# A two-MLP attention kernel on one core: buffers of the second MLP and of the state rows placed by SBUF zones, the first forms moved into the state rows, two PSUM banks exchanged, the last block by rows

## The chip, the core and the metric

The kernel runs on one core of a Trainium2 chip. The metric is the device time of one execution in microseconds (us). Engine names are those of the profile: PE is the TensorE matmul, PEld its weight load, DVE is VectorE, ACT is ScalarE, SP is SyncE, whose queue (SPq) issues nearly all DMAs of this kernel, strictly in its order.

## What is computed

The reference is an attention between 512 token rows and 32 state rows per batch and head (8 batches, 8 heads of 64), then two MLPs over all 4608 rows (4096 token rows, 512 per batch, and 256 state rows, 32 per batch): the first with relu squared, the second with elu.

```python
    scores = scale * np.matmul(x, state.transpose(0, 1, 3, 2))
    a = softmax(scores)                                # over the 32 state rows
    xread = np.matmul(a, state)
    a2 = softmax(scale * np.matmul(state, x.transpose(0, 1, 3, 2)))   # over the 512 rows
    sread = np.matmul(a2, x)
    x = rows of concat([xread, sread])                 # 4608 x 512
    x = np.maximum(x @ w_in, 0.0) ** 2 @ w_out         # 512 -> 2048 -> 512
    h = x @ w_in2
    return np.where(h > 0.0, h, np.exp(np.minimum(h, 0.0)) - 1.0) @ w_out2
```

## The kernel before

Everything is kept transposed: features on the 128 partitions, rows along the free axis, a block being the 512 rows of one batch. An fp32 product is made of three fp32r matmuls, HI·LO, HI·HI and LO·HI, where a tile's HI part is a rounded copy (ACT, L163) and LO the remainder (DVE, L164); `split` makes both, and `mm3` or `product` issues the three (L158 to L160, or L43). TensorE is the engine that is nearly always busy.

The stages in order. Attention and the first MLP for six single blocks (`block`, L475 to L502): 16 steps, each with h = W1·x in one of two PSUM banks, relu and square on ACT, and two steps later four accumulations `acc`; at the block's end four copies `acc` to `o` in turn by ACT (L501) and DVE (L499), in two buffers, each followed by its DMA to `x2d` in DRAM (L502). `mp` (L329) are the small products that give a block its first operand, split into `m_..` tiles. Then one pair of blocks, 6 and 7 (`pair`, from L617): h of both in 32 steps, its banks alternating between two PSUM pools (`ps_y`, `ps_x`), then seven products with four fewer-than-eight sub-products (`out_products`, L47 to L101) whose weights `wr` are streamed by L614.

Then the state rows of the first MLP (L678 to L717): 256 columns, 16 steps `i` in a period each of 24 matmuls of 256 columns. A step makes h from `w1s[i]` (12 matmuls), relu (ACT L694), the square (DVE L696), the split `gs`, the split of `w1s[i+2]` (two ACT and two DVE operations), and two steps later 12 matmuls into `acc`. At the end four copies `acc` to `o` in two buffers (L714 DVE, L716 ACT), each with a DMA to `x2d[8]` (L717).

Then the second MLP in four pairs of blocks (n = 0 to 3). `load_xr` (L758) brings two blocks back from `x2d`, 1024 KB each; `x_forms` makes seven operands `xf` from them, each a split (ACT and DVE over 1024 columns), with four additions or subtractions on DVE (L776, L779, L784 and one more); `first_product` (L788 to L838) is made of groups of six matmuls named X, Y or Z, each with a weight tile `wr` of 256 KB brought by L751 out of a pool of 12; `second_product` follows by `out_products`. Last comes `state_block` (L882 to L930): the second MLP for the 256 state rows, `hs` and `as` products, the `as` accumulations over 8 steps `j`, then four copies to `o` in three buffers (ACT L929, DVE L927) and four DMAs to the output (L930).

The tile scheduler orders the instructions of every engine by their dependencies and the order written; each engine and SP's queue then run strictly in that order. Buffers come from pools: a tile that takes a buffer's place waits for the last use of what was there, the landing of a DMA out of it included, and a pool that is opened in the place of a closed one waits for the users of that part of SBUF or PSUM.

Of the kernel before, what the change touches and what calls it, by code (L numbers as in the profile page):

```python
# [9 lines left out]
F32 = mybir.dt.float32  # L10
F32R = mybir.dt.float32r
# [8 lines left out]
P = 128  # L20
# [9 lines left out]
NF = 7  # L30
# [74 lines left out]
def attn_mlp_kernel(ctx: ExitStack, tc: tile.TileContext, xt, xn, st, w1, v1, w2, v2, outx, outs):  # L105
# [63 lines left out]
    if True:  # L169
# [275 lines left out]
        w1s = {}  # L445

        def split_w1(f):
            t = at_p.tile([P, 2, KC, P], F32R, name=f"w1s{f}", tag=("t", "a2t")[f % 2])
            for c in range(2):
                sl = slice(2 * c, 2 * c + 2)  # L450
                split(t[:, HI, sl], t[:, LO, sl], w1_t[f // 4, c][:, :, (f % 4) * P:(f % 4 + 1) * P])
            w1s[f] = t
# [145 lines left out]
        single.close()  # L598


        double = one.enter_context(ExitStack())
        pool = pools(double)
        gq1_p = pool("gq1", FC)
# [2 lines left out]
        eu1_p = pool("eu1", 2)  # L606
        u21_p = pool("u21", 2)
        oo1_p = pool("oo1", 2)
        ps_x, ps_y, ps_z = [pool(n, 2, space=bass.MemoryType.PSUM) for n in ("psx1", "psy1", "psz1")]
        def weight1(j, f):  # L610
            t = wr1_p.tile([P, 2, 256], F32R, name="wr", tag="wr")
            src = {1: lambda: v1d[j][:, :, :256], 2: lambda: v1d[j + HF][:, :, :256],
# [4 lines left out]
        def pair(b0, bg):  # L617

            g = {q: [] for q in (11, 12, 21, 22)}
            for s in range(2 * FC):  # L620
                b, f = b0 + s // FC, s % FC
                ps = (ps_y, ps_x)[f % 2].tile([P, S], F32, name="h1", tag="yx"[f % 2])
                s1_x(b, ops[b], f, ps)
                t = g[(11, 12, 21, 22)[s // HF]]
                if f % 2 == 0:
                    t.append(gq1_p.tile([P, 2, S], F32, name="g1", tag="gq"))
                h = t[-1][:, f % 2]
                pace[:] = [nc.scalar.activation(out=h, in_=ps, func=AF.Relu)]
# [46 lines left out]
            pair(b, bg)  # L675


        v1s = {}  # L678

        def load_v1(f):  # L680
            if f < FC:
                v1s[f] = gq1_p.tile([P, 2, DM], F32R, name="v1s", tag="gq")
                nc.sync.dma_start(out=v1s[f].bitcast(F32), in_=v1d[f])

        for f in range(4):
            load_v1(f)
        op = operand_s()
        gs = {}
        for i in range(FC + LAG):
            if i < FC:  # L690
                ps = ps_x.tile([P, NST], F32, name="h", tag="x")
                s1_s(op, i, ps)
                r = eu1_p.tile([P, NST], F32, name="r", tag="eu")
                nc.scalar.activation(out=r, in_=ps, func=AF.Relu)  # L694
                g = u21_p.tile([P, NST], F32, name="g", tag="u2")
                nc.vector.tensor_tensor(out=g, in0=r, in1=r, op=ALU.mult)  # L696
                t = gs[i] = gp1_p.tile([P, 2, NST], F32R, name="gs", tag="gp")
                split(t[:, HI], t[:, LO], g)
                if i + 2 < FC:
                    split_w1(i + 2)  # L700
                load_v1(i + 4)
            f = i - LAG
            if f < 0:
                continue
            if f == 0:
                acc = [p.tile([P, NST], F32, name="acc", tag=c) for p, c in ((ps_y, "y"), (ps_z, "z")) for _ in range(2)]
            w, t = v1s.pop(f), gs.pop(f)
            for k in range(KC):
                sl = slice(k * P, (k + 1) * P)
                mm3(acc[k], (w[:, HI, sl], w[:, LO, sl]), (t[:, HI], t[:, LO]), f == 0, f == FC - 1)  # L710
        for k in range(KC):
# [3 lines left out]
            else:  # L715
                nc.scalar.activation(out=o, in_=acc[k], func=AF.Copy)  # L716
            nc.sync.dma_start(out=x2d[B][:, k], in_=o)  # L717
        double.close()
        one.close()


    pool2 = lambda name, bufs, **kw: ctx.enter_context(tc.tile_pool(name=name, bufs=bufs, reuse_waits="tile", **kw))
    xr_p = pool2("xr", 2)
    xf_p = pool2("xf", NF)
    wr_p = pool2("wr", 12)
    eu_p = pool2("eu", 5)
    u2_p = pool2("u2", 2)
    gq_p = pool2("gq", FC)
    gp_p = pool2("gp", 3)
    oo_p = pool2("oo", 3)  # L730
    ps_y = pool2("psy", 2, space=bass.MemoryType.PSUM)
    ps_z = pool2("psz", 3, space=bass.MemoryType.PSUM)
    ps_x = pool2("psx", 3, space=bass.MemoryType.PSUM)
    act, tt = nc.scalar.activation, nc.vector.tensor_tensor
    DM1, DM2 = slice(0, 2), slice(2, 4)

    def elu(h, out):

# [10 lines left out]
    def weight(name, j, f):  # L749
        t = wr_p.tile([P, 2, 256], F32R, name="wr", tag="wr")  # L750
        nc.sync.dma_start(out=t.bitcast(F32), in_=wf[name, j][:, f - 1])  # L751
        return t

    xf, xr = {}, {}

    def load_xr(b):
        xr[b] = xr_p.tile([P, KC, S], F32, name=f"xr{b}", tag="xr")
        nc.sync.dma_start(out=xr[b], in_=x2d[b])  # L758

    def x_forms(n):  # L760

        t1, t2 = xr[2 * n], xr[2 * n + 1]
        a11, a12, a21, a22 = t1[:, DM1], t1[:, DM2], t2[:, DM1], t2[:, DM2]

        def put(f, src):
            t = xf[n, f] = xf_p.tile([P, 2, 2, S], F32R, name=f"xf{n}_{f}", tag="xf")
            split(t[:, HI], t[:, LO], src)

        put(1, a11)
        yield  # L770
        put(2, a12)
        yield
        tt(out=a21, in0=a21, in1=a22, op=ALU.add)
        put(5, a21)
        yield
        tt(out=a11, in0=a21, in1=a11, op=ALU.subtract)  # L776
        put(6, a11)
        yield
        tt(out=a21, in0=a22, in1=a11, op=ALU.subtract)  # L779
        put(7, a21)  # L780
        yield
        put(4, a22)
        yield
        tt(out=a12, in0=a12, in1=a11, op=ALU.subtract)  # L784
        put(3, a12)
        yield

    def first_product(n, g):  # L788

# [76 lines left out]
    def prepare_s():  # L866

        raw = xr_p.tile([P, KC, NST], F32, name="xsr", tag="xr")
        nc.sync.dma_start(out=raw, in_=x2d[B])
        for i in range(2):  # L870
            load_plain(*order[i])
        yield
        xs[0] = xr_p.tile([P, 2, KC, NST], F32R, name="xs", tag="xr")
        split(xs[0][:, HI], xs[0][:, LO], raw)
        yield
        for i in range(4):
            split_plain(*order[i])
            if i + 2 < len(order):
                load_plain(*order[i + 2])
            yield  # L880

    def state_block(prepared):  # L882
# [14 lines left out]
        for i in range(HF + 2):  # L897
            if i < HF:
                w = plain.pop(("w2", i))
                ps = ps_x.tile([P, 2, NST], F32, name="hs", tag="x")  # L900
                for r in range(2):
                    for d in range(2):
                        sl = [slice(r * 256 + k * P, r * 256 + (k + 1) * P) for k in range(2)]
                        product(nc, ps[:, r], [(w[:, HI, d, x], w[:, LO, d, x]) for x in sl],
                                [(xs[0][:, HI, 2 * d + k], xs[0][:, LO, 2 * d + k]) for k in range(2)],
                                r == 1 and d == 1, r == 0 and d == 0)
                g = gq_p.tile([P, 2, NST], F32, name="gsf", tag="gq")
                elu(ps, g)
                t = gs[i] = gq_p.tile([P, 2, 2, NST], F32R, name="gss", tag="gq")
                split(t[:, HI], t[:, LO], g)  # L910
                refill()
            j = i - 2
            if j < 0:
                continue
            if j == 0:
                acc = [p.tile([P, NST], F32, name="as", tag=c) for p, c in ((ps_y, "y"), (ps_z, "z")) for _ in range(2)]
            w, t = plain.pop(("v2", j)), gs.pop(j)
            for r in range(2):
                for m in range(KC):
                    sl = slice(m * P, (m + 1) * P)  # L920
                    product(nc, acc[m], [(w[:, HI, r, sl], w[:, LO, r, sl])], [(t[:, HI, r], t[:, LO, r])],
                            j == HF - 1 and r == 1, j == 0 and r == 0)
            refill()
        for m in range(KC):
            o = oo_p.tile([P, NST], F32, name="o", tag="o")
            if m % 2:
                nc.vector.tensor_copy(out=o, in_=acc[m])  # L927
            else:
                act(out=o, in_=acc[m], func=AF.Copy)  # L929
            nc.sync.dma_start(out=outs[m * P:(m + 1) * P, :], in_=o)  # L930

    for b in range(2):
        load_xr(b)
    for _ in x_forms(0):
        pass
    for n in range(B // 2):
        g = {}
# [51 lines left out]
```

## Time and profile before

| | us |
|---|---|
| three runs | 1344.03, 1344.10, 1342.67; median 1344.03 |
| the profiled execution, its own time | 1342.72 |
| its span, first to last instruction | 1340.9 |
| PE busy in it | 1321.0 |
| mean granted clock of PE | 0.999 |

A row of the timeline has the start, the duration, the engine, the line, the operation, output and input tiles, and in brackets how long the engine was idle before it and what ended that. Matmuls overlap, so the cadence is read from starts: the 512-column ones follow each other by 0.227 us, the 256-column ones by 0.12 us.

### The profile page before, as it was taken

The numbers are of one execution on the slowest core, as the hardware profiler recorded it, in microseconds if no ns is written. First come the engines' busy times: TensorE is split into PE (matmuls) and PEld (weight loads), VectorE is DVE, ScalarE is ACT, GpSimd is POOL, SyncE is SP. The second block draws the span as 40 slices with busy tenths as digits, with TensorE's granted clock in tenths as the row PEclk, the third lists the DMA queues.
The fourth block names the chain that finished last, engine by engine and source line by source line (L and its number), as shares of the span: only waits on it lengthen the run. The fifth ranks groups of instructions, "written<-read, shape, count | busy, mean of one in ns | idle before, by whom it ended". The sixth has DMA issues, their size and how long they took to land.

```text
span 1340.9 us, 19689 instructions
## 1 busy us (share of the span) xinstructions
PE 1321.0 (99%) x7064; PEld 1056.0 (79%) x7064; DVE 914.5 (68%) x1373; ACT 836.6 (62%) x1417; POOL 0.7 (0%) x6
## 2 busy tenths in 40 slices
PE   8999999999999999999999999999999999999998
PEld 6567777777677777788978888888888888888898
DVE  6986758686867645775476974579646884568644
ACT  5996657776766547654466743676446843666444
POOL 0000000000000000000000000000000000000000
PEclk9999999999999999999999999999999999999999
DMA  7998866676765203488086777678777677778733
GB/s 272 318 303 318 308 239 235 249 280 221 283 230 212 97 24 103 141 269 311 9 294 195 224 240 238 193 194 260 219 225 193 208 208 223 209 211 279 227 107 100
DMA packets 127729, 290.72 MB, mean 217 GB/s; under 512 B 13840, under 2 KB 22032, under 8 KB 124560
## 3 DMA queue, kind: packets, MB, share of 16 engines
q1 hardware_dynamic: 127632, 289.46, 66.4%
q8 instruction: 56, 0.92, 0.3%
q14 instruction: 41, 0.34, 0.1%
HBM read 212.86 MB, written 76.55 MB: 216 GB/s over the span
## 4 chain that ended last, share of the span: by engine, by line
PE 88%; ACT 3%; DMA 3%; DVE 3%; issue 1%; SPq 0%; DVEq 0%; ACTq 0%
PE x L43 16%; PE X L43 13%; PE z L43 8%; PE Z L43 6%; PE acc L158 6%; PE acc L160 6%; PE acc L159 6%; PE h L158 4%; PE h L159 4%; PE y L43 4%; PE h L160 4%; PE Y L43 3%; PE mp L329 2%; PE hs L43 2%; PE as L43 2%
## 5 line engine op out<-in xcount | busy, mean ns | idle before, releaser
L163 ACT ACTIVATE gp<-g 128x1024 fp32r<-128x1024 f32 (+1 forms) x168 | 153.9, 916 | 144.0 <-PE x L43 68.4
L164 DVE TENSOR_TENSOR gp<-g,gp 128x1024 fp32r<-128x1024 f32 (+1 forms) x168 | 175.0, 1046 | 96.0 <-ACT gp L163 94.3
L43 PE MATMUL x<-gp,wr 128*128 128x512 f32 x960 | 223.6, 390 | 0.0
L43 PEld LDWEIGHTS x<-gp,wr 128*128 128x128 f32 x960 | 179.6, 188 | 39.6 <-ACT eu L71 1.9
L43 PE MATMUL X<-xf,wr 128*128 128x512 f32 x768 | 186.6, 390 | 0.0
L43 PEld LDWEIGHTS X<-xf,wr 128*128 128x128 f32 x768 | 143.4, 188 | 31.6 <-ACT u L746 1.3
L158 PE MATMUL acc<-gs,v 128*128 128x512 f32 x384 | 155.0, 404 | 3.6 <-DVE gs L472 3.6
L160 PE MATMUL acc<-gs,v 128*128 128x512 f32 x384 | 150.3, 391 | 0.0
L159 PE MATMUL acc<-gs,v 128*128 128x512 f32 x384 | 149.9, 390 | 0.0
L43 PE MATMUL z<-gp,wr 128*128 128x512 f32 x480 | 110.4, 389 | 0.0
L742 DVE SCALAR_TENSOR_TENSOR g<-r,g 128x512 f32<-128x512 f32 x96 | 63.9, 689 | 65.8 <-ACT r L741 65.8
L158 PE MATMUL h<-at,m 128*128 128x512 f32 x256 | 102.1, 399 | 3.0 <-ACT r L467 1.9
L43 PEld LDWEIGHTS z<-gp,wr 128*128 128x128 f32 x480 | 90.1, 188 | 18.7
L158 PEld LDWEIGHTS acc<-gs,v 128*128 128x128 f32 x384 | 72.0, 188 | 40.9 <-issue 15.9
L159 PE MATMUL h<-at,m 128*128 128x512 f32 x256 | 100.6, 393 | 0.0
L160 PE MATMUL h<-at,m 128*128 128x512 f32 x256 | 99.7, 391 | 0.0
L467 ACT ACTIVATE r<-h 128x512 f32<-128x512 f32 x96 | 57.3, 597 | 64.5 <-PE h L160 64.3
L43 PE MATMUL Z<-xf,wr 128*128 128x512 f32 x384 | 97.4, 389 | 0.0
L740 ACT ACTIVATE r<-g 128x512 f32<-128x512 f32 x96 | 57.5, 625 | 57.5 <-DVE g L819 40.4
L472 DVE TENSOR_TENSOR gs<-g,gs 128x512 fp32r<-128x512 f32 x96 | 66.1, 689 | 29.5 <-ACT gs L471 28.5
L160 PEld LDWEIGHTS acc<-gs,v 128*128 128x128 f32 x384 | 72.1, 188 | 17.3 <-issue 1.7
L159 PEld LDWEIGHTS acc<-gs,v 128*128 128x128 f32 x384 | 72.2, 188 | 15.2 <-issue 1.7
(142 smaller groups left out, 2137.5 us busy)
## 6 DMA issues: line engine op xcount, KB each, us to landing
wr<-f_v SPq DMA_DIRECT2D x256, 256.0 KB, 3.1
wr<-f_w SPq DMA_DIRECT2D x224, 256.0 KB, 3.0
f_v<-wf SPq DMA_DIRECT2D x40, 512.0 KB, 3.4
raw_w<-in_w_dram SPq DMA_DIRECT2D x32, 512.0 KB, 5.1
raw_v<-in_v_dram SPq DMA_DIRECT2D x32, 512.0 KB, 5.1
f_w<-wf SPq DMA_DIRECT2D x24, 512.0 KB, 3.3
xt<-in_xt_dram SPq DMA_DIRECT2D x8, 1024.0 KB, 7.8
xn<-in_xn_dram SPq DMA_DIRECT2D x8, 1024.0 KB, 5.9
```

What stands on the lines that cost most here:

```text
L43: nc.tensor.matmul(ps, wk[a], xk[b], start=start and k == 0 and i == 0, stop=last and k == len(w) - 1 and i == 2, skip_group_check=True)
L158: mm(ps, w[HI], x[LO], start=first, stop=False)
L159: mm(ps, w[HI], x[HI], start=False, stop=False)
L160: mm(ps, w[LO], x[HI], start=False, stop=last)
L163: copy = nc.scalar.activation(out=hi, in_=src, func=AF.Copy)
L164: nc.vector.tensor_tensor(out=lo, in0=src, in1=hi.bitcast(F32), op=ALU.subtract)
L329: mm(ps[e][32 * k:32 * k + 32, :], st_t[b][r, k, :], x(k, r), start=True, stop=True)
L467: pace[:] = [nc.scalar.activation(out=r, in_=ps, func=AF.Relu)]
L472: nc.vector.tensor_tensor(out=gs[:, LO], in0=g, in1=gs[:, HI].bitcast(F32), op=ALU.subtract)
L740: act(out=r, in_=h, func=AF.Relu, scale=-1.0)
L742: nc.vector.scalar_tensor_tensor(out=out, in0=r, scalar=-1.0, in1=h, op0=ALU.add, op1=ALU.max)
```

## The change

Four things are done.

1. Pools. `w1s` of the state rows gets a pool of its own at the right end of SBUF, opened before the pair, instead of two buffers of the attention; the state rows get a stage `rows` with own pools (`eu2`, `u22`, `oo2`, six `v1s` buffers instead of the pair's sixteen, `gs` in the `m` buffers; PSUM pools in the order y, x, z). The second MLP's pools are opened in another order, `xr`, `xf` and `gp` at the right end.
2. `load_xr(0)`, `load_xr(1)` and the seven steps of `x_forms(0)` are called inside the loop over the state rows, a form at every second step from i = 4; before they stood behind that loop.
3. The pair's h goes to `ps_z` and `ps_y`, and its PSUM pools are opened as y, x, z instead of x, y, z.
4. In the last step j of `state_block` the loop runs by rows of the output: all six matmuls of `acc[0]`, then those of `acc[1]`, and so on; `o` takes buffers of the `eu` pool (5) instead of `oo` (3).

```diff
         def split_w1(f):
-            t = at_p.tile([P, 2, KC, P], F32R, name=f"w1s{f}", tag=("t", "a2t")[f % 2])
+            t = w1s_p.tile([P, 2, KC, P], F32R, name=f"w1s{f}", tag="w1s")
...
+        w1s_p = right("w1s", 2)
         double = one.enter_context(ExitStack())
...
-        ps_x, ps_y, ps_z = [pool(n, 2, space=bass.MemoryType.PSUM) for n in ("psx1", "psy1", "psz1")]
+        ps_y, ps_x, ps_z = [pool(n, 2, space=bass.MemoryType.PSUM) for n in ("psy1", "psx1", "psz1")]
...
-                ps = (ps_y, ps_x)[f % 2].tile([P, S], F32, name="h1", tag="yx"[f % 2])
+                ps = (ps_z, ps_y)[f % 2].tile([P, S], F32, name="h1", tag="zy"[f % 2])
...
+        double.close()
+        xr_p = right("xr", 2)
+        xf_p = right("xf", NF)
+        rows = one.enter_context(ExitStack())
+        v1_p = rows.enter_context(tc.tile_pool(name="v1s", bufs=6, side="right", reuse_waits="tile"))
+        pool = pools(rows)
+        eu1_p = pool("eu2", 2)
+        u21_p = pool("u22", 2)
+        oo1_p = pool("oo2", 2)
+        ps_y, ps_x, ps_z = [pool(n, 2, space=bass.MemoryType.PSUM) for n in ("psy2", "psx2", "psz2")]
...
+        for b in range(2):
+            load_xr(b)
+        forms = x_forms(0)
         for i in range(FC + LAG):
...
-                t = gs[i] = gp1_p.tile([P, 2, NST], F32R, name="gs", tag="gp")
+                t = gs[i] = m_p.tile([P, 2, NST], F32R, name="gs", tag="m")
...
+            if i > 3 and i % 2 == 0:
+                next(forms, None)
...
-        double.close()
+        rows.close()
         one.close()
...
+    pool = pools(ctx)
+    xs_p = pool("xs", 1)
+    gq_p = pool("gq", FC)
+    eu_p = pool("eu", 5)
+    oo_p = pool("oo", 3)
+    u2_p = pool("u2", 2)
+    wr_p = pool("wr", 12)
+    gp_p = right("gp", 3)
...
-            for r in range(2):
-                for m in range(KC):
-                    sl = slice(m * P, (m + 1) * P)
...
+            last = j == HF - 1
+            for i in range(2 * KC):
+                r, m = (i % 2, i // 2) if last else divmod(i, KC)
...
-            o = oo_p.tile([P, NST], F32, name="o", tag="o")
+            o = eu_p.tile([P, NST], F32, name="o", tag="eu")
```

What stands in a row on TensorE where the pair begins: `acc` is the last accumulation of block 5, `mp6_1` the operand products of block 6, `h1` the first h of the pair. Before:

```order
L160 MATMUL acc_4531<-gs_5091,v1_15_1068 128x512
L329 MATMUL mp6_1_0_5208<-w1_10_318,st6_3894 32x512 [waits PE_49]
L329 MATMUL mp6_1_1_5209<-w1_10_318,st6_3894 32x512 [waits PE_49]
L329 MATMUL mp6_1_0_5208<-w1_10_318,st6_3894 32x512
L329 MATMUL mp6_1_1_5209<-w1_10_318,st6_3894 32x512
L329 MATMUL mp6_1_0_5208<-w1_11_373,st6_3894 32x512
L329 MATMUL mp6_1_1_5209<-w1_11_373,st6_3894 32x512
L329 MATMUL mp6_1_0_5208<-w1_11_373,st6_3894 32x512
L329 MATMUL mp6_1_1_5209<-w1_11_373,st6_3894 32x512
L158 MATMUL h1_5189<-at6_4722,m6_00_4984 128x512 [waits Activation_49]
```

The same place after the change:

```order
L160 MATMUL acc_4531<-gs_5091,v1_15_1068 128x512
L158 MATMUL h1_5196<-at6_4722,m6_00_4984 128x512
L159 MATMUL h1_5196<-at6_4722,m6_00_4984 128x512
L160 MATMUL h1_5196<-at6_4722,m6_00_4984 128x512
L158 MATMUL h1_5196<-at6_4722,m6_01_4987 128x512
L159 MATMUL h1_5196<-at6_4722,m6_01_4987 128x512
L160 MATMUL h1_5196<-at6_4722,m6_01_4987 128x512
L329 MATMUL mp6_1_0_5215<-w1_10_318,st6_3894 32x512 [waits PE_49]
L329 MATMUL mp6_1_1_5216<-w1_10_318,st6_3894 32x512 [waits PE_49]
L158 MATMUL h1_5206<-at6_4722,m6_00_4984 128x512 [waits Activation_49]
L159 MATMUL h1_5206<-at6_4722,m6_00_4984 128x512
```

The first h now stands ahead of the operand products and waits for no copy; the second stands between two of the products and the remaining six, and waits for ACT.

What stands in a row on SP where the state rows end and the second MLP begins: `x2d8` are the four DMAs of the state rows' `o`, `wr` the weights of `first_product` for n = 0, `xr2` and `xr3` the blocks of n = 1. Before:

```order
L751 DMA wr_7015<-f_w20_2009 128x512 [waits DMAHW2_49,DVE_49]
L751 DMA wr_7026<-f_w20_2009 128x512 [waits DMAHW3_49,DVE_49,PE_49]
L751 DMA wr_7040<-f_w20_2009 128x512 [waits DMAHW4_49]
L751 DMA wr_7048<-f_w20_2009 128x512 [waits DMAHW5_49]
L751 DMA wr_7059<-f_w21_2056 128x512 [waits DMAHW6_49]
L717 DMA x2d8_131<-o_6912 128x256 [waits DMAHW7_49,Activation_49]
L717 DMA x2d8_131<-o_6915 128x256 [waits DMAHW0_49,DVE_49]
L751 DMA wr_7069<-f_w20_2009 128x512 [waits DMAHW1_49]
L751 DMA wr_7080<-f_w21_2056 128x512 [waits DMAHW2_49]
L751 DMA wr_7094<-f_w21_2056 128x512 [waits DMAHW3_49]
L717 DMA x2d8_131<-o_6918 128x256 [waits DMAHW4_49,Activation_49]
```

After:

```order
L697 DMA xr2_7044<-x2d2_125 128x2048 [waits DVE_49,Activation_49]
L697 DMA xr3_7046<-x2d3_126 128x2048 [waits DVE_49,Activation_49]
L771 DMA x2d8_131<-o_6984 128x256 [waits DMAHW4_49,Activation_49]
L771 DMA x2d8_131<-o_6987 128x256 [waits DMAHW5_49,DVE_49]
L771 DMA x2d8_131<-o_6990 128x256 [waits DMAHW6_49,Activation_49]
L771 DMA x2d8_131<-o_6993 128x256 [waits DMAHW7_49,DVE_49]
L803 DMA wr_7053<-f_w20_2009 128x512 [waits DMAHW0_49]
L803 DMA wr_7064<-f_w20_2009 128x512 [waits DMAHW1_49]
L803 DMA wr_7078<-f_w20_2009 128x512 [waits DMAHW2_49]
```

All weights of the second MLP now stand behind the four DMAs of the state rows' `o`; before, five stood ahead of them and three more between the second and the third.

What stands in a row on TensorE at the same place. Before:

```order
L160 MATMUL acc<-gs,v1s 128x256
L43 MATMUL Y<-xf_2_6984,wr 128x512 [waits DMAHW3_49,DVE_49,PE_49]
L43 MATMUL Y<-xf_2_6984,wr 128x512 [waits Activation_49]
L43 MATMUL Y<-xf_2_6984,wr 128x512 x4
L43 MATMUL Z<-xf_5_6988,wr 128x512 [waits DMAHW4_49,DVE_49]
L43 MATMUL Z<-xf_5_6988,wr 128x512 [waits Activation_49]
L43 MATMUL Z<-xf_5_6988,wr 128x512 x4
L43 MATMUL Y<-xf_2_6984,wr 128x512 [waits DMAHW2_49,PE_49]
L43 MATMUL X<-xf_1_6981,wr 128x512 x6
```

After:

```order
L160 MATMUL acc<-gs,v1s 128x256
L43 MATMUL X<-xf_1_6512,wr 128x512 [waits DMAHW0_49]
L43 MATMUL X<-xf_1_6512,wr 128x512 x5
L43 MATMUL Y<-xf_2_6593,wr 128x512 [waits DMAHW1_49,PE_49]
L43 MATMUL Y<-xf_2_6593,wr 128x512 x5
L43 MATMUL Z<-xf_5_6675,wr 128x512 [waits DMAHW2_49,Activation_49]
```

The first group is now X, and it waits for a weight's DMA alone; before, the first Y also waited for the forms on DVE and ACT.

## Rows read from the trace of the kernel before

**Rows 1.** Page of the profile: busy us, share of the span, instructions by engine.

```profile
PE 1321.0 (99%) x7064; PEld 1056.0 (79%) x7064; DVE 914.5 (68%) x1373; ACT 836.6 (62%) x1417; POOL 0.7 (0%) x6
```

**Rows 2.** Waits of PE: what for, us in total, times, the longest.

```profile
PE Y L43 <- DMA wr<-f_w: 1.9, 1, 1.9
```

**Rows 3.** Timeline where the pair begins: PE and ACT.

```profile
497.87 0.60 ACT L501 ACTIVATE o<-acc 128x512 f32<-128x512 f32 x1 [3.63 <-PE acc L160]
...
499.80 1.09 PE L329 MATMUL mp<-w,st 64*32 64x512 f32 x16
501.14 0.60 ACT L501 ACTIVATE o<-acc 128x512 f32<-128x512 f32 x1 [2.68 <-DMA x2d<-o]
...
501.79 0.51 PE L158 MATMUL h<-at,m 128*128 128x512 f32 x1 [0.90 <-ACT o L501]
```

**Rows 4.** Timeline of PE: operand products, then an acc that follows them.

```profile
479.15 1.09 PE L329 MATMUL mp<-w,st 64*32 64x512 f32 x16
480.17 0.50 PE L158 MATMUL acc<-gs,v 128*128 128x512 f32 x1
```

**Rows 5.** Groups by line, 660 to 690; count, busy us, mean ns.

```profile
L164 DVE TENSOR_TENSOR xf<-xr,xf 128x1024 fp32r<-128x1024 f32 x7 | 8.4, 1220 | 2.3 <-ACT xf L163 2.3
...
L163 ACT ACTIVATE xf<-xr 128x1024 fp32r<-128x1024 f32 x7 | 7.2, 1051 | 0.5 <-DVE xr L776 0.3 <-DVE xr L779 0.2
```

**Rows 6.** Window in the state rows: busy us of PE, PEld, DVE, ACT, POOL.

```profile
640.00:660.00 20.00, 20.00 (x169) 20.00 (x168) 10.02 (x28) 9.10 (x28) 0.00 (x0) 1.00 0.05 14
```

**Rows 7.** Timeline of the state rows' end: PE.

```profile
674.34 0.28 PE L160 MATMUL acc<-gs,v1s 128*128 128x256 f32 x1
...
674.82 0.39 PE L158 MATMUL acc<-gs,v1s 128*128 128x256 f32 x1 [0.20 <-DVE gs L164]
```

**Rows 8.** Timeline of SP's queue there.

```profile
675.89 0.80 SPq L717 DMA_DIRECT2D x2d<-o  x2
```

**Rows 9.** Timeline into the second MLP: ACT, DVE and PE.

```profile
675.48 0.38 ACT L716 ACTIVATE o<-acc 128x256 f32<-128x256 f32 x1
...
675.84 0.42 DVE L714 COPY o<-acc 128x256 f32<-128x256 f32 x1
...
676.36 1.55 PE L43 MATMUL Y<-xf,wr 128*128 128x512 f32 x6
...
677.92 0.39 ACT L716 ACTIVATE o<-acc 128x256 f32<-128x256 f32 x1 [2.06 <-PE Y L43]
...
681.20 0.47 PE L43 MATMUL Y<-xf,wr 128*128 128x512 f32 x1 [1.93 <-DMA wr<-f_w]
```

**Rows 10.** Timeline of PE: first products: n = 0's end, then n = 1's.

```profile
758.10 2.20 PE L43 MATMUL x<-gp,wr 128*128 128x512 f32 x9
...
831.61 1.52 PE L43 MATMUL X<-xf,wr 128*128 128x512 f32 x6
...
910.96 2.43 PE L43 MATMUL x<-gp,wr 128*128 128x512 f32 x10
```

**Rows 11.** DMA issues, 655 to 657: us to landing with no other transfer.

```profile
wr<-f_w SPq DMA_DIRECT2D x1, 256.0 KB, 2.7
```

**Rows 12.** Windows: busy us of PE, PEld, DVE, ACT, POOL; granted clock; DMA.

```profile
2.00:3.00 1.00, 1.00 (x6) 1.00 (x6) 0.00 (x0) 0.01 (x1) 0.00 (x0) 1.00 0.65 233
...
7.00:8.00 1.00, 1.00 (x10) 1.00 (x9) 0.00 (x0) 0.00 (x0) 0.00 (x0) 1.00 0.91 315
...
679.00:681.20 2.20, 0.27 (x2) 0.03 (x1) 2.20 (x4) 2.00 (x3) 0.00 (x0) 1.00 0.97 331
...
1339.00:1340.00 1.00, 0.00 (x0) 0.00 (x0) 0.00 (x0) 0.00 (x0) 0.00 (x0) 0.50 0.39 131
```

**Rows 13.** Timeline of the end.

```profile
1335.77 0.88 PE L43 MATMUL as<-gss,pl 128*128 128x256 f32 x6
...
1336.02 2.62 SPq L930 DMA_DIRECT2D out_dram<-o  x4
...
1337.86 0.42 DVE L927 COPY o<-as 128x256 f32<-128x256 f32 x1 [1.46 <-DMA out_dram<-o]
```

More of the change, by code (lines that the diff above doesn't have):

```diff
@@ L598, in attn_mlp_kernel @@
         single.close()
+        right = lambda name, bufs: ctx.enter_context(tc.tile_pool(name=name, bufs=bufs, side="right", reuse_waits="tile"))
+        right("edge", 1).tile([P, 8], F32, name="edge", tag="edge")
+        w1s_p = right("w1s", 2)
         double = one.enter_context(ExitStack())
@@ L675, in attn_mlp_kernel, with load_xr, x_forms, put @@
             pair(b, bg)
+        double.close()
[8 more added lines that the diff above has]
+        ps_y, ps_x, ps_z = [pool(n, 2, space=bass.MemoryType.PSUM) for n in ("psy2", "psx2", "psz2")]
+        xf, xr = {}, {}
+        DM1, DM2 = slice(0, 2), slice(2, 4)
+        def load_xr(b):
+            xr[b] = xr_p.tile([P, KC, S], F32, name=f"xr{b}", tag="xr")
+            nc.sync.dma_start(out=xr[b], in_=x2d[b])
+        def x_forms(n):
+            t1, t2 = xr[2 * n], xr[2 * n + 1]
+            a11, a12, a21, a22 = t1[:, DM1], t1[:, DM2], t2[:, DM1], t2[:, DM2]
+            def put(f, src):
+                t = xf[n, f] = xf_p.tile([P, 2, 2, S], F32R, name=f"xf{n}_{f}", tag="xf")
+                split(t[:, HI], t[:, LO], src)
+            put(1, a11)
+            yield
+            put(2, a12)
+            yield
+            nc.vector.tensor_tensor(out=a21, in0=a21, in1=a22, op=ALU.add)
+            put(5, a21)
+            yield
+            nc.vector.tensor_tensor(out=a11, in0=a21, in1=a11, op=ALU.subtract)
+            put(6, a11)
+            yield
+            nc.vector.tensor_tensor(out=a21, in0=a22, in1=a11, op=ALU.subtract)
+            put(7, a21)
+            yield
+            put(4, a22)
+            yield
+            nc.vector.tensor_tensor(out=a12, in0=a12, in1=a11, op=ALU.subtract)
+            put(3, a12)
+            yield
         v1s = {}
@@ L681, in load_v1 @@
             if f < FC:
-                v1s[f] = gq1_p.tile([P, 2, DM], F32R, name="v1s", tag="gq")
+                v1s[f] = v1_p.tile([P, 2, DM], F32R, name="v1s", tag="v1s")
                 nc.sync.dma_start(out=v1s[f].bitcast(F32), in_=v1d[f])
@@ L717, in attn_mlp_kernel @@
             nc.sync.dma_start(out=x2d[B][:, k], in_=o)
-        double.close()
+        rows.close()
         one.close()
[L722 to L733, printed above, removed]
+    pool = pools(ctx)
[6 more added lines that the diff above has]
+    gp_p = right("gp", 3)
+    ps_y = pool("psy", 2, space=bass.MemoryType.PSUM)
+    ps_z = pool("psz", 3, space=bass.MemoryType.PSUM)
+    ps_x = pool("psx", 3, space=bass.MemoryType.PSUM)
     act, tt = nc.scalar.activation, nc.vector.tensor_tensor
-    DM1, DM2 = slice(0, 2), slice(2, 4)
     def elu(h, out):
@@ L752, in weight @@
         return t
[L754 to L786, printed above, removed]
     def first_product(n, g):
@@ L872, in prepare_s @@
         yield
-        xs[0] = xr_p.tile([P, 2, KC, NST], F32R, name="xs", tag="xr")
+        xs[0] = xs_p.tile([P, 2, KC, NST], F32R, name="xs", tag="xs")
         split(xs[0][:, HI], xs[0][:, LO], raw)
@@ L917, in state_block @@
             w, t = plain.pop(("v2", j)), gs.pop(j)
-            for r in range(2):
-                for m in range(KC):
-                    sl = slice(m * P, (m + 1) * P)
-                    product(nc, acc[m], [(w[:, HI, r, sl], w[:, LO, r, sl])], [(t[:, HI, r], t[:, LO, r])],
-                            j == HF - 1 and r == 1, j == 0 and r == 0)
+            last = j == HF - 1
+            for i in range(2 * KC):
+                r, m = (i % 2, i // 2) if last else divmod(i, KC)
+                sl = slice(m * P, (m + 1) * P)
+                product(nc, acc[m], [(w[:, HI, r, sl], w[:, LO, r, sl])], [(t[:, HI, r], t[:, LO, r])],
+                        last and r == 1, j == 0 and r == 0)
             refill()
         for m in range(KC):
-            o = oo_p.tile([P, NST], F32, name="o", tag="o")
+            o = eu_p.tile([P, NST], F32, name="o", tag="eu")
             if m % 2:
@@ L930, in state_block @@
             nc.sync.dma_start(out=outs[m * P:(m + 1) * P, :], in_=o)
-    for b in range(2):
-        load_xr(b)
-    for _ in x_forms(0):
+    for _ in forms:
         pass
```

## The prediction, made before the changed kernel was run

> **What bounds the kernel now.** I read the busy times first: TensorE is busy for 1321.0 of 1340.9 us [rows 1], so only two things count, TensorE's work, which the change leaves as it is, and TensorE's idle places. The list of PE's waits says which of these the change reaches: the largest is 1.9 us for a weight `wr` of the second MLP [rows 2], and a copy `o` holds it for 0.9 [rows 3]. The timeline then gives each place: where the pair begins [rows 3], where the state rows end [rows 7 to 9] and the kernel's last microseconds [rows 13]. DVE and ACT matter only where they are ahead of one of these.
>
> **The pair's first h.** Before, the operand products `mp` start at 499.80 and take 16 slots; the next such run, 479.15 to 480.17, shows 1.02 us to the matmul behind it [rows 4], so h could have started at 500.82. It started at 501.79, because its bank waited for ACT's second `o`, which itself waited for a DMA out of the first [rows 3]: 0.97 us lost. After, the first h goes to a bank that no copy holds and stands ahead of `mp`; the second waits for the `o` of 497.87, done at 498.48, long before. The late copy then holds up a later h that is not yet wanted. Against this: `mp` is now broken in two, one more switch between the two kinds of matmul. The `acc` behind such a run lasts 0.50 [rows 4], 0.27 over a slot of 0.227; I count 0.3. ACT also gets the splits of `w1s[0]` and `[1]` here, four of some 0.4 us, which may cost a later h as much as one of them. I take a gain of 0.5, between 0 (both eat it) and 0.97.
>
> **The state rows.** Seven forms and two loads come in among 16 periods. A period of 24 matmuls at 0.12 us is 2.88 us. DVE was busy 10.02 and ACT 9.10 of 20 us there [rows 6], so 1.44 and 1.31 us of a period: about half is free. The forms need of DVE seven splits and four additions at 1.22 us, 13.4 us, and of ACT seven at 1.05, 7.4 us [rows 5]. They come in eight periods, 23.0 us: ACT 7.4 + 8 × 1.31 = 17.9 fits; DVE 13.4 + 8 × 1.44 = 24.9 overflows by 1.9 us. That backlog costs TensorE nothing as long as `gs` has slack: h of step i is wanted as `gs` two periods later, 5.76 us, of which the chain of relu, square and the two halves of the split takes four operations of about 0.4, so some 4 us are left. The two loads of 1024 KB have the DMA engines nearly to themselves, 0.05 busy in that window [rows 6]. So I put the forms at nothing, covered by DVE's free half; what they cost when that cover is gone is the second rival. What they save is one stall: at 674.82 an `acc` waited for a `gs` that stood behind a form of 1.22 us on DVE [rows 7]. The matmul before it started at 674.34 [rows 7] in a cadence of 0.12: 0.48 − 0.12 = 0.36 us. The forms are done by then after the change: −0.36.
>
> **Into the second MLP.** Here the change moves most, and not the way its placement reads. Before, the first Y starts at 676.36, the slot after the last `acc`; call it T0 [rows 9]. PE idles 1.93 us at 681.20 for a weight. The whole cost of the transition: from T0 to the same `x` group the first product takes 758.10 − 676.36 = 81.74 us, for n = 1 it takes 910.96 − 831.61 = 79.35 [rows 10], so 2.39 us.
>
> After, all `wr` stand behind the four DMAs of the state rows' `o` on SP's queue, and SP executes in order. The `o` have two buffers, so the third and fourth copies wait for the first and second DMA to land. I take these times from the same place in the trace. The first copy starts at 675.48, its DMA is issued at 675.89 [rows 8, 9], and ACT's next copy starts at 677.92: 2.03 us from issue to reuse; at the kernel's end the same chain takes 1337.86 − 1336.02 = 1.84 [rows 13]. The second copy runs from 675.84 to 676.26 on DVE; its issue starts at about 676.30. The fourth copy, on DVE, can therefore start 1.84 to 2.03 us later, at 678.14 to 678.33, and takes 0.42; its issue takes SP 0.3 to 0.4 (two took 0.80 [rows 8]), so SP comes to the first `wr` at 678.9 to 679.2. A `wr` of 256 KB alone lands 2.7 us after issue [rows 11]. TensorE gets its first X at 681.6 to 682.0: idle for 5.2 to 5.6 us from T0, and I take 5.4. Later weights are issued every 0.4 us [rows 8] and wanted every 1.36 (six matmuls of 0.227), so I expect no second wait. The difference is 5.4 − 2.39 = **+3.0 us** (2.8 to 3.3).
>
> **The clock after that gap.** With TensorE idle for 1.93 us the granted clock stayed at 1.00; after the last matmul of the kernel it was 0.50, the low level (1.2 GHz), by 1339 [rows 12], the last matmul having ended at 1336.65 [rows 13]. At the kernel's start, out of idleness, six idle matmuls went by in the microsecond from 2, ten in that from 7 [rows 12]; the recorded clock is 1.00 in both, so I go by the counts. If all of 1 to 7 ran at 0.6 of the rate, 6 × 0.4 = 2.4 us were lost; at half rate 3.0. After the gap the same loss, or none if the clock holds: 0 to 3.0. I take 2.4, because the start is the only restart that this trace has.
>
> The Trainium skill speaks against the change here: in its page "TensorE: Matmul & The Clock Gate", section "HAM oscillation — how this bites in real kernels", a TensorE left waiting for DMAs falls to half rate and the burst behind the wait starts cold. Its example has 1.67 us of throttled time for each such wait, by an estimate from that page 0.84 us lost, with which the time would be 1345.2. The clock of 0.50 at the end of the trace agrees; a restart behind a gap in the middle is not in it.
>
> **The last block.** The last matmul ends at 1336.65, but the fourth copy waited for a landing until 1337.86 [rows 13]. With free buffers and the first three copies ended by then (`acc[0]` now ends 18 matmuls earlier instead of 9) the fourth starts at about 1336.7, and its DMA lands that much earlier: −1.17, between −1.0 and −1.2.
>
> **Everything else** I put at nothing: six `v1s` buffers instead of sixteen still load four steps ahead, 11.5 us, and the DMA engines are free there [rows 6]; other pools and zones change addresses; the pair's seven products take their banks in another order, without a wait that this trace shows near. What would cost is a late transfer, in the second rival.
>
> **The sum.** −0.5 − 0.36 + 3.0 − 1.17 = +1.0 us, and with the clock's 2.4, **+3.4**. The profiled execution took 1342.72 and the median of three is 1344.03; I add to the middle of the two, 1343.4: **1346.8**.
>
> **Rivals.**
> - *The clock holds through the gap.* For: 1.93 us of idling left it at 1.00 [rows 12]; a low stretch might be short too. Against: 0.50 at the end of the trace. It gives 1343.4 + 1.0 = 1344.4, not slower.
> - *DVE falls behind in the state rows, on top of the gap: slower still.* The backlog of 1.9 us leaves about 2 us of slack. If the forms come in closer than one in a period, or if an operand block lands late and holds everything behind it on DVE's queue, TensorE loses each microsecond beyond that slack. From about 4 us of backlog it decides; at 2 us beyond, 1348.7. For: DVE in order, and the additions wait for the loads. Against: the DMA engines' emptiness [rows 6].
> - *The change does what its placement reads as: weights and forms are there when the state rows end.* Then the 2.39 us vanish too: −0.5 − 0.36 − 2.39 − 1.17 = −4.4, so 1339.0, faster. It needs `wr` issued before the third and fourth `o`, or their DMAs much quicker than 1.84 us. Against: the order of SP's queue, printed above. This is where I would be most wrong.
>
> **How the numbers follow.** A measurement of this kernel can tell about 0.2%, 2.7 us, from no change: 1341.3 to 1346.7. The forecast (gap, low clock) has 0.57, about half of it above that bound: slower 0.30, same 0.27. The clock holding has 0.20: same 0.18, slower 0.02. DVE or a load late 0.13: slower 0.12, same 0.01. The weights in time 0.07: faster. Something small elsewhere 0.03: same. Together faster 0.07, same 0.49, slower 0.44. The range takes in the clock at nothing and at 3.0 with the other terms at their ends, and part of the second rival: 1343.2 to 1349.0; left out are the third rival and the worse half of the second.
>
> **What would show it.** In the profile after, PE's waits name X, not Y, behind a `wr`, once, at 5.2 to 5.6 us, and SP's timeline has the fourth `x2d` issue 2.2 to 2.5 us after the last `acc` and the first `wr` right behind it; the granted clock is 0.50 at the end of that gap and some us beyond. The wait for `gs` at the end of the state rows is gone and none has come in its place; no h of the pair waits for ACT's `o`; the last copy starts within 0.1 us of the last matmul. I am wrong if X starts within 2 us of the last `acc`, if the clock stays at 1.00, or if PE waits for `gs` inside the state rows.

## The result: slower, by more than twice what was forecast

| | before | after |
|---|---|---|
| median, us | 1344.07 (1342.67 to 1345.3) | 1350.42 (1348.83 to 1352.51) |
| ratio after to before | | 1.0051, 95% interval 1.0038 to 1.0064 |
| profiled execution, its own time | 1342.72 | 1350.49 |
| its span | 1340.9 | 1348.7 |

The change costs 6.35 us by the medians; I had said 2.8 against the median of before (1346.8) and a range up to 1349.0. The time lies outside it.

The profile after, first PE's busy time on the page, which answers to [rows 1] (before 1321.0):

```profile
PE 1324.5 (98%) x7064; PEld 1053.2 (78%) x7064; DVE 914.9 (68%) x1373; ACT 837.4 (62%) x1417; POOL 0.7 (0%) x6
```

PE's waits, which answer to [rows 2]: what for, us in total, times, longest.

```profile
PE X L43 <- DMA wr<-f_w: 6.6, 1, 6.6
...
PE acc L158 <- DVE gs L164: 0.9, 1, 0.9
```

The wait for a weight, 1.9 us before, is 6.6, on X as foretold; the wait for `gs` that was to go (0.2 us of idling before) is 0.9. The wait of h for ACT's `o` is not in the list any more.

The timeline into the second MLP after, SP's queue, ACT, DVE and PE, answers to [rows 8, 9]:

```profile
674.99 3.12 SPq L771 DMA_DIRECT2D x2d<-o  x4
...
675.28 0.28 PE L160 MATMUL acc<-gs,v1s 128*128 128x256 f32 x1
...
676.90 0.39 ACT L770 ACTIVATE o<-acc 128x256 f32<-128x256 f32 x1 [1.94 <-DMA x2d<-o]
...
677.33 0.42 DVE L768 COPY o<-acc 128x256 f32<-128x256 f32 x1 [1.99 <-DMA x2d<-o]
...
678.16 21.93 SPq L803 DMA_DIRECT2D wr<-f_w  x23
...
682.14 2.93 PE L43 MATMUL X<-xf,wr 128*128 128x512 f32 x6 [6.58 <-DMA wr<-f_w]
```

The chain is the one of the prediction: the third and fourth copies wait for the first two DMAs to land, SP comes to the first weight at 678.16, 2.77 us after the slot behind the last `acc` (675.39). The weight then takes 3.98 us until X starts, not 2.7.

The windows there, the granted clock behind the five busy times, answer to [rows 12]:

```profile
679.00:680.00 1.00, 0.00 (x0) 0.00 (x0) 0.00 (x0) 0.00 (x0) 0.00 (x0) 1.00 0.74 90
680.00:681.00 1.00, 0.00 (x0) 0.00 (x0) 0.00 (x0) 0.00 (x0) 0.00 (x0) 0.55 0.94 244
...
686.00:687.00 1.00, 1.00 (x4) 0.73 (x4) 0.00 (x0) 0.00 (x0) 0.00 (x0) 0.53 1.05 402
687.00:688.00 1.00, 1.00 (x6) 0.82 (x5) 0.52 (x1) 0.00 (x0) 0.00 (x0) 1.00 1.05 406
```

The clock fell while PE idled and was low into 687, as forecast. The first products of n = 1 and n = 2 start, before and after, at

```profile
984.47 1.52 PE L43 MATMUL X<-xf,wr 128*128 128x512 f32 x6
```

(before; n = 1 at 831.61 [rows 10]) and

```profile
838.72 1.54 PE L43 MATMUL X<-xf,wr 128*128 128x512 f32 x6
...
992.99 1.30 PE L43 MATMUL X<-xf,wr 128*128 128x512 f32 x5
```

A pair of blocks in the middle of the second MLP takes 984.47 − 831.61 = 152.86 us before and 992.99 − 838.72 = 154.27 after, with the same instructions in the same order, PE busy throughout and the clock at 1.00. Nothing in the prediction spoke of that. The account of the two profiled spans, from the starts of the stages' matmuls, in us:

| stage | before | after | difference |
|---|---|---|---|
| up to the last `acc` of block 5 (unchanged code) | 499.48 | 498.99 | −0.49 |
| the pair, h | 53.79 | 53.93 | +0.14 |
| the pair, products | 76.56 | 76.49 | −0.07 |
| state rows, first h to last `acc` | 46.41 | 45.87 | −0.54 |
| last `acc` to first group of the second MLP | 0.12 | 6.86 | +6.74 |
| n = 0 | 155.25 | 156.58 | +1.33 |
| n = 1, 2, 3 | 152.86, 152.86, 130.81 | 154.27, 154.27, 131.95 | +3.96 |
| last block | 68.50 | 66.35 | −2.15 |
| last matmul to the end | 4.29 | 3.13 | −1.16 |
| sum | | | +7.76 |

### The profile page after: what moved, and what is told of

It is laid out like the page before. It is cut to its first block, busy times and chain, and to the rows that moved or that the text cites. A ratio compares the mean times of both kernels' runs of the same rounds, so it can differ in the third digit from the quotient of the medians.

```text
span 1348.7 us, 19679 instructions
## 1 busy us (share of the span) xinstructions
PE 1324.5 (98%) x7064; PEld 1053.2 (78%) x7064; DVE 914.9 (68%) x1373; ACT 837.4 (62%) x1417; POOL 0.7 (0%) x6
## 4 chain that ended last, share of the span: by engine, by line
PE 86%; ACT 4%; DMA 4%; DVE 3%; issue 1%; SPq 0%; ACTq 0%; DVEq 0%
PE x L43 16%; PE X L43 13%; PE z L43 8%; PE Z L43 7%; PE acc L158 6%; PE acc L160 5%; PE acc L159 5%; PE y L43 4%; PE h L158 4%; PE h L159 4%; PE h L160 4%; PE Y L43 3%; PE mp L329 2%; PE as L43 2%; PE hs L43 1%
## 5 line engine op out<-in xcount | busy, mean ns | idle before, releaser
L43 PE MATMUL X<-xf,wr 128*128 128x512 f32 x768 | 189.4, 394 | 6.6 <-DMA wr<-f_w 6.6
L158 PEld LDWEIGHTS acc<-gs,v 128*128 128x128 f32 x384 | 72.0, 188 | 40.8 <-issue 15.9
L160 PEld LDWEIGHTS acc<-gs,v 128*128 128x128 f32 x384 | 72.1, 188 | 17.4 <-issue 1.7
L43 PEld LDWEIGHTS Z<-xf,wr 128*128 128x128 f32 x384 | 72.1, 188 | 15.8
```

Source lines behind the costliest of these rows:

```text
L43: nc.tensor.matmul(ps, wk[a], xk[b], start=start and k == 0 and i == 0, stop=last and k == len(w) - 1 and i == 2, skip_group_check=True)
L158: mm(ps, w[HI], x[LO], start=first, stop=False)
L160: mm(ps, w[LO], x[HI], start=False, stop=last)
```

## The experiments

**What changes the pace.** Reading the starts of successive matmuls to the nanosecond: in the second MLP before they follow each other by 227, 227, 226 ns, after by 229, 232, 226. The last block's (256 columns) go from 120 to 113, the state rows' `acc` from 120 to mostly 113. The buffers' byte addresses in their partition follow from the order and the sizes of the kernel's pools: before, `wr` 75904, `xf` 18560, `gp` 180352, all multiples of 128; after, `wr` 96384 (a multiple of 128), `xf` 147392 and `gp` 122816 (both 64 beyond one). The changed kernel opens a tile `edge` of 32 bytes at the right end ahead of all else there, and every pool behind it at that end holds tiles of whole multiples of 128 bytes; so this tile is likely what puts them 64 off, though no run leaves it out. So a theory on the start within 128 bytes, against one on SBUF regions.

**Edit 1, 64 bytes ahead of `wr`:**

```diff
+    pool("pad", 1).tile([P, 16], F32, name="pad", tag="pad")
     wr_p = pool("wr", 12)
```

> The changed kernel with 64 bytes put in front of the weight buffers wr of the second MLP and nothing else: the order on every engine is the same. Theory A, that a matmul's pace hangs on where its two operands start within 128 bytes (wr at a multiple of 128, xf and gp 64 beyond, in the changed kernel; all alike in the kernel before): the second MLP's 512-column matmuls go back from 229/232/226 ns to 227/227/226, a pair of blocks from 154.3 to 152.9 us, the whole 5 to 6 us shorter, about 1345. Theory B, that it hangs on which regions of SBUF the operands lie in: no buffer changes region, so 229/232/226 stay and the time is 1350.4. The gap into the second MLP (6.6 us) stays by both.

Measured: 1345.21 us (ratio to before 1.0006, 0.9997 to 1.0016). n = 1 starts and ends at

```profile
837.62 1.52 PE L43 MATMUL X<-xf,wr 128*128 128x512 f32 x6
...
990.51 1.52 PE L43 MATMUL X<-xf,wr 128*128 128x512 f32 x6
```

so 152.89 us; the gap stays (6.37 us). 64 bytes give 5.2 us back, and no buffer changed its region: theory A stands for the second MLP, B falls.

**Edit 2, the `o` DMAs of the state rows from ACT's queue:**

```diff
-            nc.sync.dma_start(out=x2d[B][:, k], in_=o)
+            nc.scalar.dma_start(out=x2d[B][:, k], in_=o)
         rows.close()
```

> The changed kernel with the four DMAs of the state rows' o issued from ScalarE's queue instead of SyncE's, so that the weights of the second MLP stand directly behind the last x block on SyncE. If SyncE's order made the 6.6 us gap: X starts in the slot behind the last acc, the clock stays at 1.00, and 6.6 + 2.35 us are gone, about 1341.5. If the transfers themselves or the buffers' release were behind it, X still waits several us and the time stays near 1349. The 229/232/226 ns of the second MLP stay by every theory.

Measured: 1343.87 us, the profiled execution 1341.83 against 1350.49. X follows the last `acc` in the next slot, and the clock stays at 1.00 in every window there:

```profile
673.64 0.28 PE L160 MATMUL acc<-gs,v1s 128*128 128x256 f32 x1
673.75 1.54 PE L43 MATMUL X<-xf,wr 128*128 128x512 f32 x6
```

SP's order made the gap. n = 0 takes 154.52 us, against 156.58 with the low clock behind the gap, so the clock cost 2.06. Gap and clock are 8.8 us by the stages; the medians differ by 6.6, less than the expected 8.9, and the ratio to before is 0.9996 (0.9987 to 1.0006): as fast as before, not faster. That the profiled executions differ by 8.7 is in part chance. In this one the unchanged first stage ran 1.3 us shorter, and the last block 1.75 longer (68.10 against 66.35) with the same buffers at the same addresses. From the first `hs` on, the second MLP's last matmuls, some 95, follow each other by 233 ns instead of 229, and most of the last block's by 118 instead of 113. PE in 20 us of the last block, here:

```profile
1310.00:1330.00 20.00, 20.00 (x172) 20.00 (x172) 11.55 (x13) 12.02 (x18) 0.00 (x0) 1.00 0.38 128
```

and in the changed kernel, at the same clock of 1.00:

```profile
1320.00:1340.00 20.00, 20.00 (x179) 20.00 (x178) 11.73 (x14) 12.34 (x18) 0.00 (x0) 1.00 0.39 127
```

So where buffers start does not fix the pace by itself when weights and operand start unlike; what set off the slower one here isn't shown.

**Edit 3, both.**

> Both edits, the 64 bytes in front of wr and the o DMAs from ScalarE's queue. If the two losses are independent, the gains add: 5.6 + 8.9 us below the changed kernel, about 1336, faster than the kernel before by 8 us. If the pace theory falls, as e2 alone: 1341.5.

Measured: 1336.74 us, ratio 0.9946 (0.9933 to 0.9958): faster than both kernels. The gains at least add: 5.2 and 6.6 us by the medians, 13.7 measured; by the profiled executions 5.1 and 8.7, and 14.6. Part of the surplus is that this profile has neither the wait for `gs` nor the slower last block of edit 2's. Nothing is left of the gap, three first groups in a row (a later Y waits 0.5 us for its weight):

```profile
674.36 1.54 PE L43 MATMUL X<-xf,wr 128*128 128x512 f32 x6
675.73 1.52 PE L43 MATMUL Y<-xf,wr 128*128 128x512 f32 x6
677.09 1.52 PE L43 MATMUL Z<-xf,wr 128*128 128x512 f32 x6
```

**Edit 4, the kernel before with the same 64 bytes ahead of `wr`** (there ahead of `eu`, `u2`, `gq`, `gp` and `oo` too):

> The kernel before with 64 bytes put in front of wr; the buffers behind it (gq, gp) move by 64 with it, xf and the last block's pl and xs don't. Theory A: second product (wr and gp alike) stays at 226.7 ns; first product now has wr at 64 and xf at 0 beyond a multiple of 128, the reverse of the changed kernel: 226.7 if only the other sense is slow, 229 if any difference is, which makes 2 us in 1344; the last block's as product has weights pl at 0 and gss at 64, the one sense not seen yet with 256 columns. Theory B: nothing changes anywhere, 1344.0.

Measured: 1351.8 us, ratio 1.0053 (1.0041 to 1.0065): an unaltered order made slower by 64 bytes. The first products, weights 64 beyond and operand at 0, run at 233, 233, 234 ns, slower than the 229 of the changed kernel's sense (I had put 226.7 or 229, and 2 us at most). That the sense decides between 229 and 233 isn't shown: edit 2's profile has 233 in the other sense too. The second products, both 64 beyond, run at 227. n = 1 takes 988.51 − 833.50 = 155.01:

```profile
833.50 1.56 PE L43 MATMUL X<-xf,wr 128*128 128x512 f32 x6
...
988.51 1.56 PE L43 MATMUL X<-xf,wr 128*128 128x512 f32 x6
```

The last block's `as`, weights at 0 and operand 64 beyond, go from 120 to 118 ns.

**Edit 5, one operand alone:** the kernel before with 64 bytes ahead of `gp` (and of `oo` behind it, which no matmul reads).

```diff
+    pool2("pad", 1).tile([P, 16], F32, name="pad", tag="pad")
     gp_p = pool2("gp", 3)
```

> The kernel before with 64 bytes in front of the operand gp of the second products alone (gp goes to 64 beyond a multiple of 128, its weights wr stay at 0; xf, xs, gss, pl stay). Theory A: only the second products slow down, from 227/227/226 to 229/232/226 ns, 0.7 us for each of four, the first products keep 226.7: 1346.8. If a shift of any buffer perturbs all stages, the first products change too. Theory B: nothing changes, 1344.0.

Measured: 1346.02 us, ratio 1.0020 (1.0011 to 1.0030). The second products' `x`, `y`, `z` run at 229, 232, 226 ns, the first products' at 227, 227, 226; n = 1 takes 988.48 − 834.86 = 153.62 us, 0.76 more, where theory A had 0.7:

```profile
834.86 1.31 PE L43 MATMUL X<-xf,wr 128*128 128x512 f32 x5
...
988.48 1.53 PE L43 MATMUL X<-xf,wr 128*128 128x512 f32 x6
```

**Edit 6, the last block's operands:** edit 3 with the pad ahead of `xs` instead of `wr`, which moves `xs` and `gss` by 64 and leaves `wr` where edit 3 has it.

> The kernel of e3_both with the 64 bytes put in front of xs instead of wr: wr stays where it is in e3_both, the operands xs and gss of the last block go to 64 beyond a multiple of 128, where their weights pl are. Theory A: its 256-column matmuls go from 113 to 118 ns back to 120, the last block from 66.4 to 68.5 us, everything else as e3_both. Theory B: 66.4.

Measured: the last block takes 68.45 us, its matmuls 120 ns again (one profile, 1337.69 us). PE in 20 us of it, where the changed kernel has 179 matmuls (edit 2):

```profile
1310.00:1330.00 20.00, 20.00 (x169) 20.00 (x168) 11.11 (x13) 10.62 (x16) 0.00 (x0) 1.00 0.27 83
```

With 256 columns it is the other way round: weights and operand that start alike are slower than unlike.

**Edit 7, the first MLP by the same rule:** edit 3 with `at` and `sts` moved to multiples of 128.

```diff
     at_p = pool("attn", 1)
+    sn_p = pool("sn", 1)
...
-            mx = sm_p.tile([P, 2], F32, name=f"mx{b}", tag="mx")
-            z2 = sm_p.tile([P, 2], F32, name=f"z2{b}", tag="z2")
+            mx = sn_p.tile([P, 2], F32, name=f"mx{b}", tag="mx")
+            z2 = sn_p.tile([P, 2], F32, name=f"z2{b}", tag="z2")
```

> The kernel of e3_both with two tiles of 8 bytes moved behind the attention's pools, so that the operands at and sts (first MLP, single and pair blocks, and state rows) start at a multiple of 128 bytes instead of 64 beyond; m stays at a multiple of 128, w1s at 64 beyond. Theory A: the 768 h matmuls of 512 columns lose their 229/232/226 pattern for 227/227/226, 2.2 ns each, 1.7 us; the state rows' h of 256 columns, operand at 0 and weights at 64, go from 117 to 120 ns toward 113 to 118, up to 0.8 us. About 1334.5 against 1336.7. Theory B (regions): nothing moves region, 1336.7.

Measured: 1337.67 us, ratio 0.9958 (0.9945 to 0.9971): no gain, a miss. The h's 229/232/226 gave way to a mixture led by 227, 0.25 ns quicker in the mean, but the `acc` that stand between them, moved by nothing, went from mostly 227 to a mixture of 226 to 236, 1 ns slower. In the state rows `acc` went from mostly 113 to 118 ns, their addresses unmoved, while h went to 118. So theory A, made for one pair of operands, doesn't cover loops in which two kinds of matmul alternate. Either what one kind is fed changes the other's pace, or, in the state rows, `acc` took the second of the two paces that edit 2's last block shows at unmoved addresses; the runs don't tell these apart.

**Edit 8, four `o` buffers in the state rows of the changed kernel:**

```diff
-        oo1_p = pool("oo2", 2)
+        oo1_p = pool("oo2", 4)
```

> The changed kernel with four o buffers in the state rows instead of two: SyncE's order is the same, but no copy waits for a landing. By the chain of the prediction the first weight is then issued about 1.1 us after the last acc instead of 2.8, and the gap falls by about that, from 6.9 to about 5.1 us; the rest of the gap is the weights' landing, near 3.9 us with twelve of them and the o in flight. If the copies' buffers are not in the chain, it stays at 6.9.

Measured: the gap is 4.74 us instead of 6.86 (one profile, 1349.27 us):

```profile
675.36 1.78 SPq L771 DMA_DIRECT2D x2d<-o  x4
...
677.19 3.77 SPq L803 DMA_DIRECT2D wr<-f_w  x8
680.39 0.92 PEld L43 LDWEIGHTS X<-xf,wr 128*128 128x128 f32 x3 [4.66 <-DMA wr<-f_w]
```

Of the 2.12 us, 1.34 are the buffers': SP comes to the first weight 1.43 us after the slot behind the last `acc` (675.76), not 2.77 (I had put 1.1). The other 0.78 is a shorter landing, 680.39 − 677.19 = 3.20 here, which the buffers need not have made: edit 1's profile, with the changed kernel's order, has 3.49 between the same two events where the changed kernel has 3.98.

**Edit 9, only the pair's banks and the last block, in the kernel before** (parts 3 and 4 of the diff):

> The kernel before with only the two small edits, the pair's h on the other banks and the last block by rows with five o buffers. By the prediction's terms: 0.5 us at the pair's start (0 to 0.97) and 1.17 at the end, about 1342.3 against 1344.0; the wait of h for ACT's o gone, the last copy within 0.1 us of the last matmul. The rival is that the bank order of the pair costs back what the first h gains: 1342.8.

Measured: 1342.4 us, ratio 0.9996 (0.9986 to 1.0005), so the whole time does not tell the 1.7 us that I expected from nothing; the stages do. Last matmul to end: 3.13 us against 4.29, so −1.16. The pair's h takes 53.93 against 53.79, no gain, and the pair's products 77.92 against 76.56 in this profile. The banks did not make that: the profiles of edits 4 and 5, where the pair is unchanged, have 77.99 and 77.94. In all three one y waits 0.9 to 1.0 us for its `gp` from DVE, here

```profile
PE y L43 <- DVE gp L164: 1.0, 1, 1.0
```

and in the profiles of the kernel before and of the changed kernel (76.49) none does.

**Edit 10, only the DMA queue, in the kernel before** (edit 2 there):

> The kernel before with one edit, the state rows' four o DMAs issued from ScalarE's queue instead of SyncE's; forms, pools and banks as before. If SyncE's order alone made the 1.93 us wait of Y, all twelve weights land in time, the transition's 2.39 us shrink to near 0.5 and the time falls by about 2 us, to 1341.7; the forms behind the state rows then cost nothing worth moving them for. If the forms on VectorE and ScalarE are the next thing late, an X or Y waits for xf instead, for 1 us or more, and the time stays within 1 us of before.

Measured: 1343.7 us, ratio 1.0007 (0.9999 to 1.0016). Y and Z no longer wait for a weight, but the next X does, for a copy:

```profile
677.81 1.52 PE L43 MATMUL X<-xf,wr 128*128 128x512 f32 x6
...
680.31 0.38 ACT L716 ACTIVATE o<-acc 128x256 f32<-128x256 f32 x1 [5.74 <-DMA x2d<-o]
...
681.17 1.65 PE L43 MATMUL X<-xf,wr 128*128 128x512 f32 x6 [1.84 <-DVE o L714]
```

ACT's second `o` waits for the DMA out of the first, which took 5.6 us to land instead of 1.9 in the kernel before, with weights under way beside it, and the forms behind it on ACT come late. Moving the forms into the state rows pays only with the weights in time, and the weights in time only with the forms moved: together n = 0 takes 153.72 us (edit 3), the forms alone 156.58 (the changed kernel), the queue alone 156.69, neither 155.25.

## Why the prediction was wrong, by its steps

- **The pair's first h: wrong in sign.** I gave −0.5; measured +0.14. The wait is gone, but the operand products are now broken in two. PE there, after, answers to [rows 3, 4]:

```profile
500.68 1.05 PE L329 MATMUL mp<-w,st 64*32 64x512 f32 x4
501.66 0.50 PE L158 MATMUL h<-at,m 128*128 128x512 f32 x1
...
503.24 1.08 PE L329 MATMUL mp<-w,st 64*32 64x512 f32 x12
504.25 0.50 PE L158 MATMUL h<-at,m 128*128 128x512 f32 x1
```

  Four of them take as long (0.98 us to the next h) as twelve (1.01) or sixteen (1.02 [rows 4]). The step that failed: "I count 0.3" for the break, read from how long one `acc` lasts and not from a run to the next start. The time belongs to the run, not to its products, so a second run cost about 1.1 us, 0.98 and two more changes between the kinds at some 0.1 (318 and 334 ns where h follows h by 229). The trace of the kernel before had this already:

```profile
87.53 1.05 PE L329 MATMUL mp<-w,st 64*32 64x512 f32 x4
88.50 0.50 PE L160 MATMUL acc<-gs,v 128*128 128x512 f32 x1
```

- **The state rows: right that no form holds PE, wrong about one addition.** I gave −0.36. The loss is 1.06 us instead of 0.36: after a start at 672.75 the next `acc` starts at 673.92, with `gs` late behind this on DVE:

```profile
671.39 1.23 DVE L712 TENSOR_TENSOR xr<-xr 128x1024 f32<-128x1024 f32 x1 [2.06 <-DMA xr<-x2d]
672.54 0.42 DVE L748 TENSOR_TENSOR g<-r 128x256 f32<-128x256 f32 x1
...
673.92 0.39 PE L158 MATMUL acc<-gs,v1s 128*128 128x256 f32 x1 [0.89 <-DVE gs L164]
```

  It is an addition for n = 1, not wanted for a long time, that stands ahead of the last `g` and waits for a block of 1024 KB that landed 7.5 us after issue (KB each, us to landing):

```profile
xr<-x2d SPq DMA_DIRECT2D x2, 1024.0 KB, 7.5
```

  That is the second rival's mechanism ("holds everything behind it on DVE's queue"); I gave it 0.13 as a case, and its price is 1.05 us against my sum. In edit 3's profile the block took 5.6 us and no `gs` waits; in those of edits 1, 2, 6, 7 and 8 it took 6.1 to 7.7 and PE idles for 0.4 to 1.1 us. It is a matter of a microsecond.
- **Into the second MLP: the mechanism right, the landing mis-sized.** Idle from T0: 6.75 us (682.14 − 675.39), forecast 5.2 to 5.6. SP came to the weight at T0 + 2.77, as said. The landing was taken as 2.7 us from a weight that flew alone [rows 11]; it took 3.98 to X's start with others issued behind it at once, and 3.49 and 3.20 in the profiles of edits 1 and 8. That the others make it longer is likely, but no run issues one weight alone there. Edits 2 and 8 show the chain.
- **The clock: right in kind, the size partly luck.** 2.4 us taken, 2.06 measured between edit 2 and the changed kernel; in edit 1, with the gap too, n = 0 takes 2.88 more than n = 1. But the 2.4 came from one start of the kernel, where 28 idle matmuls are some 0.21 us apart and not 0.11. At the start of the trace after, 13 are, which would have given about half. The clock of 0.50 to 0.55 from 680 to 687 agrees with the rule that I cited from the Trainium skill, "TensorE: Matmul & The Clock Gate", section "HAM oscillation — how this bites in real kernels"; the estimate from its example (0.84 us) was too low here.
- **The last block: right.** −1.17 said, −1.16 measured. After, the fourth copy starts on time:

```profile
1345.59 0.42 DVE L946 COPY o<-as 128x256 f32<-128x256 f32 x1 [0.93 <-PE as L43]
```

- **"Other pools and zones change addresses" at nothing: the step that failed most.** The second MLP's matmuls cost about 5.4 us more (1.41 for each of n = 0 to 2, 1.14 for n = 3), the last block 2.15 less, the state rows 1.2 less: +2.0 net in the profile. The prediction put them at nothing without a reason. Edit 1 gives 5.2 back with 64 bytes, and edit 6 takes the last block's gain away with 64 bytes; that the state rows' 1.2 has the same cause is read from the pace alone.

The terms mis-sized or missed are thus, against the sum of the prediction (+3.4): addresses +2.0, landing 1.3, the late addition 1.05, the pair's break 0.64; less 0.3 for the clock and 0.5 by which the unchanged first stage ran shorter in this execution. That makes 7.6 of the 7.8 between the two profiles.

**What stays open.** Why a start 64 bytes off slows a 512-column matmul and speeds up a 256-column one isn't shown, nor which of the two weight tiles near a matmul (its own or the next one's) meets its operand, since both always start alike here. What chooses between the two paces of unlike starts (229 and 233, 113 and 118) is open, and with it what happened in the alternating loops of edit 7.

## What to carry to other kernels

A buffer that moves costs no instruction, yet compare the pace of the same matmuls before and after from their starts, and try weights and operand of 512-column fp32r matmuls at the same start within 128 bytes; with 256 columns unlike starts were the quicker ones here. When work is moved ahead, look at what else stands on the in-order queue: here the forms were in time and the weights were queued behind four small DMAs with two buffers, and only with both in time does n = 0 get shorter. Even then the whole is as fast as before (edit 2) until the 64 bytes are put right as well (1336.74 us). A landing time taken from a transfer that flew alone, 2.7 us, was too short for one with others issued right behind it, 3.2 to 4.0.

## What the runs showed of the hardware that I had not expected

The pace of a row of like fp32r matmuls hangs on where weights and operand start within 128 bytes, with the clock at 1.00 throughout; starts at 0 and 64 were run. Alike, it is 226.7 ns with 512 columns (the kernel before, edits 1 and 3, the first products of edit 5) and 120 with 256 (the last block of the kernel before and of edit 6). Unlike, there are two paces for each: 229.0 or 233.4 with 512 columns, 113 or 118 with 256. With 512 columns and the operand alone 64 beyond, 229.0 was the rule (the changed kernel, edit 5), but edit 2's last stretch ran at 233.3; with the weights alone 64 beyond, 233.4 (edit 4). With 256 and the weights alone 64 beyond, 113 in the changed kernel, 118 in edit 2, and one after the other in the `hs` of edits 1 and 3; in the other sense 118 (edit 4). So the starts decide whether a pair leaves its even pace, but not by how much.

And a run of small `mp` matmuls took about 1 us to the next start whether it had four (0.98), twelve (1.01) or sixteen (1.02).
